# Attention and channel mix on one core: the right operands of scores and products read in another order of 16-byte lines, and the weights moved to other places

## The chip, the cores and the metric

The kernel runs on one core of a Trainium2 chip. The metric is device time in microseconds for one execution; the time given for a kernel is the median of several runs.

## The reference

There are 8 batches, 12 heads, 448 positions and a head size of 64; 12 heads of 64 make a model width of 768, and the hidden width is 1024. Everything is float32. Two stages follow one another:

```python
# attention, each element weighed by a sigmoid
scores = (q @ k.T) / sqrt(64) - log(448)
x = sigmoid(scores) @ v                     # then heads side by side: 8 x 448 x 768
# channel mix
xp = x shifted by one position
xk = mu_k * x + (1 - mu_k) * xp
xr = mu_r * x + (1 - mu_r) * xp
k  = relu(xk @ w_k)                         # 768 x 1024
v  = (k * k) @ w_v                          # 1024 x 768
r  = sigmoid(xr @ w_r)                      # 768 x 768
out = r * v
```

## The kernel before

**Attention.** Two heads share the 128 partitions, 64 each, so that there are 48 head pairs. Keys of a pair are taken in three chunks of 128 and a tail of 64. A score matmul has 128 keys of one head as weights (64 rows by 128 columns) and 448 queries as the right operand, the one that is streamed through the array; the two heads of a pair stand in the two halves of the array's rows and run side by side. Queries and keys are split in two parts each, of type fp32r (`qh`, `ql`, `kh`, `kl`), and a chunk is the sum of three terms: `kh` with `qh`, `kl` with `qh`, `kh` with `ql` (L361). The very first chunk, the key tails (L376), the products with v (L402, L412) and their tails (L426) use plain float32 operands; such a product has two records in the trace.

**Channel mix.** There are three matrix products (stage R with `w_r`, stage K with `w_k`, stage V with `w_v`), each done as seven half-size products (Strassen's scheme, `ORDER` is the order of the seven). All of their matmuls are issued from one line, L670. Weights are 128 by 128 blocks out of `slots`, seven tiles of 3072 numbers per partition, one for each of the seven; the upper part stands in the first half of a slot, the lower part in the second. Right operands are 512 (at the end of a row of blocks, 256) columns out of `rr` and later also out of `qh` and `ql`, again as an upper and a lower part (`operand`, L594 and L595). A full step takes three terms for each block of weights: upper with upper, upper with lower, lower with upper; a narrow step (`small`) takes 512 columns, in which upper and lower stand side by side, with the upper weights, and 256 with the lower ones. Weights are filled by `to_slot` (stage R) and `load_weight` (stages K and V): ACT rounds into the upper part, DVE subtracts into the lower.

**Order.** All work is put down as a list of operations with a cost and a due time. `Plan.order` runs a small list scheduler over it and writes out the instructions of each engine in the order found. Its price for a matmul is `mm(n, cols) = n * (cols / 2.4 + 13.4)` ns. Semaphores are added afterwards. `gap` reserves bytes between tiles and is otherwise unused.

The lines that place the tiles that matter here:

```python
slots = ring(base, "slot", 7, [P, 2 * WO], F32R)      # 2 * WO = 3072
rr = ring(base, "rr", 6, [P, 2, T], F32R)             # T = 512
...
qhr = ring(apool, "qh", LEAD, [P, T], F32R)
qlr = ring(apool, "ql", LEAD, [P, T], F32R)
gap(apool, "gap2", 192)
kh = ring(apool, "kh", LEAD, [P, KW], F32R)           # KW = 384
```

Of the kernel before, what the change touches and what calls it, by code (L numbers as in the profile page):

```python
# [9 lines left out]
F32R = mybir.dt.float32r  # L10
# [13 lines left out]
class Plan:  # L24
# [9 lines left out]
    def op(self, engine, cost, prio, run, reads, writes, dma=None, gate=False, opens=None):  # L34
        i = len(self.ops)
        deps = set()
        for r in reads:
            if r in self.writer:
                deps.add(self.writer[r])
        for w in writes:  # L40
            if w in self.writer:
                deps.add(self.writer[w])
            deps.update(self.readers.get(w, ()))
        for r in reads:
            self.readers.setdefault(r, []).append(i)
        for w in writes:
            self.writer[w] = i
            self.readers[w] = []
        deps.discard(i)
        self.ops.append(Op(engine, cost, prio, run, deps, dma, gate, opens))  # L50
# [58 lines left out]
def attention_then_channel_mix(  # L109
# [15 lines left out]
    nc = tc.nc  # L125
    P = 128
# [15 lines left out]
    WO = NJH * DF // 2  # L142
    SCALE = 1.0 / math.sqrt(D)
    NEG_LOG_S = -math.log(S)
    R_, K_, V_ = range(3)

    KT = (NJH, NJH, NFH)
    CW = (DM // 2, DF // 2, DM // 2)
# [18 lines left out]
    WK_PACE, WV_PACE = 1.5, 1.5  # L167
    CAST_DVE = lambda n, a: n % 2 == 1 or n == 2

    WHOLE = 1  # L170
    ZEROS = 336
    Q_FIRST = 256

    def ring(pool, name, bufs, shape, dtype):
        return [pool.tile(shape, dtype, name=f"{name}{i}") for i in range(bufs)]

    def gap(pool, name, size):
        pool.tile([P, size // 4], F32, name=name)

    base = ctx.enter_context(tc.tile_pool(name="base", bufs=1, side="left"))  # L180
    apool = ctx.enter_context(tc.tile_pool(name="apool", bufs=1, side="right"))
# [1 line left out]
    pav = psa.enter_context(tc.tile_pool(name="pav", bufs=1, space=PSUM))  # L183
    pscore = psc.enter_context(tc.tile_pool(name="pscore", bufs=1, space=PSUM, side="right"))

    slots = ring(base, "slot", 7, [P, 2 * WO], F32R)
    rr = ring(base, "rr", 6, [P, 2, T], F32R)
    ys = ring(base, "ys", 3, [P, T], F32)
    wraw = ring(base, "wraw", 2, [P, WP, 2], U32)
# [5 lines left out]
    vnr = ring(apool, "vn", 5, [P, T], F32)  # L195
    gap(apool, "gap1", 64)
    qnr = ring(apool, "qn", RAW, [P, T], F32)
    qhr = ring(apool, "qh", LEAD, [P, T], F32R)
    qlr = ring(apool, "ql", LEAD, [P, T], F32R)
    gap(apool, "gap2", 192)  # L200
    kh = ring(apool, "kh", LEAD, [P, KW], F32R)
    kl = ring(apool, "kl", LEAD, [P, KW], F32R)
    gap(apool, "gap3", 64)
# [11 lines left out]
    sc = ring(pscore, "sc", 3, [P, 2, 512], F32)  # L215
# [8 lines left out]
    def mm(n, cols):  # L224
        return n * (cols / 2.4 + 13.4)

    def act(n, sbuf=False, ptr=False):
        return 100 + 0.834 * n + 42 * sbuf + 93 * ptr

    def dve(n, fast=False, ptr=False):  # L230
        return 135 + n / (1.92 if fast else 0.96) + 61 * ptr
# [7 lines left out]
    def dma(dst, src, prio, reads, writes, e="SP"):  # L239
        ns = dst.shape[0] * math.prod(dst.shape[1:]) * 4 / 300  # L240
        q_ = nc.scalar if e == ACT else nc.sync
        op(e, 500, prio, lambda: q_.dma_start(dst, src), reads, writes, dma=ns)
# [26 lines left out]
    def convert_seven(w, t, half_rows, n, pace, at, put):  # L269
# [32 lines left out]
        combine(sub, s4, a12, s2, at + 3 * pace)  # L302
        put(2, s4, at + 3 * pace)

    def to_slot(t, n):
        def put(p, a, at):
            g = POS[p]
            hi, lo = (slots[g][:, half * KT[R_] * n + t * n:half * KT[R_] * n + (t + 1) * n] for half in range(2))
            K = ("slot", g, t)
            op(ACT, act(n, True), at, lambda: nc.scalar.copy(hi, a[0]), [a[1]], [K], gate=True)  # L310
            op(DVE, dve(n), at, lambda: nc.vector.tensor_sub(lo, a[0], hi), [a[1], K], [K + ("lo",)])
        return put
# [18 lines left out]
    def prepare(n, at):  # L331
        i = n % LEAD
        k0 = WHOLE * P if n == 0 else 0
        for src, hi, lo, a, w in ((kn[n % RAW][:, k0:KW], [t[:, k0:] for t in kh], [t[:, k0:] for t in kl], "k", KW - k0), (qn[n % RAW], qh, ql, "q", S)):
# [6 lines left out]
    half = [slice(h * D, (h + 1) * D) for h in range(2)]  # L341

    def pe(cost, go, reads, writes, at, opens=None):
        op(PE, cost, at, go, reads, writes + ["order"], opens=opens)
# [3 lines left out]
    def scores(n, c, u, at):  # L348
        i, m = n % LEAD, n % RAW
        mark = (n, c) in ((N - 1, 1), (N - 2, 2), (N - 1, 2))  # L350
        if n == 0 and c < WHOLE:
            pairs, cost, reads = ((knr[m], qnr[m]),), 752, [("kn", m), ("qn", m)]
        else:
            pairs, cost = ((kh[i], qhr[i]), (kl[i], qhr[i]), (kh[i], qlr[i])), 602
            reads = [(a, i) for a in ("kh", "kl", "qh", "ql")]

        def go(lo, hi):
            for e, (kk, qq) in enumerate(pairs):
                for h in range(2):
                    w = T if mark and e == len(pairs) - 1 else hi  # L360
                    nc.tensor.matmul(sc[u][:, h, lo:w], kk[half[h], c * P:(c + 1) * P], qq[half[h], lo:w], start=e == 0, stop=e == len(pairs) - 1, skip_group_check=mark)  # L361

        keys = [("sc", u, 0), ("sc", u, 1)]
        if (n, c) == (0, 0):

            pe(cost * Q_FIRST / S, lambda: go(0, Q_FIRST), reads, keys, at)
            pe(cost * (1 - Q_FIRST / S), lambda: go(Q_FIRST, S), reads + [("qn", 0, 1)], keys, at)
            return
        pe(cost + 2 * SWITCH * (n % 2 == c == 0), lambda: go(0, S), reads, keys, at)
# [91 lines left out]
    for t in range(KT[R_]):  # L461
        convert_seven(w_r, t, KT[R_], CW[R_], WR_PACE, WR_FROM + 4 * WR_PACE * t + 0.4, to_slot(t, CW[R_]))
# [68 lines left out]
    e = N % RAW  # L531
# [96 lines left out]
    def load_weight(stage, p, at):  # L628
        g, src = POS[p], {K_: wk_o, V_: wv_o}[stage][p]
        n = WO // 2  # L630
        for h in range(2):
            u = nw[0] % len(wop)
            nw[0] += 1
            w, W = wop[u]
            dma(w, src[:, h * n:(h + 1) * n], at, [("wo", id({K_: wk_o, V_: wv_o}[stage]), p, t) for t in range(NFH)], W)
            hi, lo = (slots[g][:, a * WO + h * n:a * WO + (h + 1) * n] for a in range(2))
            K = ("slot", g, h)
            op(ACT, act(n, True), at, lambda hi=hi, w=w: nc.scalar.copy(hi, w), W, [K])  # L638
            op(DVE, dve(n), at, lambda hi=hi, lo=lo, w=w: nc.vector.tensor_sub(lo, w, hi), W + [K], [K + ("lo",)])  # L639

    def slot_keys(g):
        return [("slot", g, h) + x for h in range(3) for x in ((), ("lo",))]
# [3 lines left out]
    def multiply(stage, s, p, i, at, cols=slice(0, T), b=None, turn=0):  # L646
        g = POS[p]
        b = b or (yb if p in (5, 6, 3) else xb)[i]
        c = cols.stop - cols.start
        rs_ = used[stage, s, p]  # L650
        w = CW[stage]
        small = PAIRS[s][1] < T

        def go():
            n = len(rs_)

            def left(t, a):
                return slots[g][:, a * n * w + t * w + i * P:a * n * w + t * w + (i + 1) * P]

            if small:  # L660

                a = turn ^ (p in (1, 6, 3))
                terms = [(left(t, a), r[0], (T, SMALL)[a]) for t, r in enumerate(rs_)]
            else:
                terms = [(left(t, a), r[e][:, cols], c) for t, r in enumerate(rs_) for a, e in ((0, 0), (0, 1), (1, 0))]
            for e, (l, r, m) in enumerate(terms):
                nc.tensor.matmul(b[0][:, :m], l, r[:, :m], start=bool(p in (0, 4) and e == turn == 0), stop=e == len(terms) - 1 and bool(turn or not small), skip_group_check=True)  # L670

        cost = mm(len(rs_), (T, SMALL)[turn ^ (p in (1, 6, 3))]) if small else mm(3 * len(rs_), c)
        op(PE, cost, at, go, [k for r in rs_ for k in r[2:]] + slot_keys(g), [b[1]])
# [87 lines left out]
    for step, (stage, s, p) in enumerate(steps):  # L761
# [6 lines left out]
        small = PAIRS[s][1] < T  # L768
        for i in range(rows if small else 0):
            multiply(stage, s, p, i, at + unit * i / (2 * rows))  # L770
        for i in range(rows):
# [9 lines left out]
            if step == len(steps) - 3 and i == rows - 1:  # L781
                a, b = yb[i], yb[NFH - 1]
# [45 lines left out]
```

## Time and profile before

| | |
|---|---|
| median of 3 runs | 803.23 us (803.14 to 803.63) |
| span of the profiled execution, first to last instruction | 801.9 us |
| TensorE matmul busy | 797.8 us, 99% |
| TensorE weight load busy | 598.8 us, 75% |
| VectorE busy | 639.7 us, 80% |
| ScalarE busy | 496.0 us, 62% |
| mean granted TensorE clock | 0.999 of full speed |

The profiled execution is one of its own beside the three timed ones; only its span is recorded, and the median of the timed runs is 1.3 us above it. Busy time of an engine is the union of its instructions. Matmuls overlap one another in the records, since each is recorded from its issue to its last result: what one matmul takes from the next is the distance of their starts.

### The profile page before, as it was taken

What the parts mean: (1) busy time and instruction counts of PE and PEld (TensorE: products, weight loads), DVE (VectorE), ACT (ScalarE), POOL (GpSimd) and SP (SyncE); (2) the same over time, 40 slices, a digit from 0 to 9 for tenths busy, and PEclk for the clock granted to TensorE, in tenths of its full rate; (3) what the DMA queues carried; (4) which work ended last, traced back from release to release, by engine and by line L of the source; (5) the groups of instructions that cost most, each with busy time, mean ns of one, the idle gap of its engine ahead of it and who ended that gap; (6) DMA issues with size and microseconds to landing.
All of it is one profiled execution on the core that took longest, in us unless ns stands there. A gap on an engine that the chain in (4) does not pass through costs nothing.

```text
span 801.9 us, 14343 instructions
## 1 busy us (share of the span) xinstructions
PE 797.8 (99%) x4935; PEld 598.8 (75%) x4935; DVE 639.7 (80%) x1210; ACT 496.0 (62%) x870; POOL 2.9 (0%) x33
## 2 busy tenths in 40 slices
PE   9999999999999999999999999999999999999998
PEld 5555555555556888888888888888888888888887
DVE  4889888898898998899987974668597585677955
ACT  6788888877785555568766464567773434345431
POOL 0000000000000000000000000000000000000000
PEclk9999999999999999999999999999999999999999
DMA  8977978789887967668877772445775564457505
GB/s 276 282 262 243 304 242 275 254 274 340 295 293 272 313 236 218 228 238 257 277 243 223 243 256 87 162 151 155 226 243 179 172 184 131 132 166 253 186 23 176
DMA packets 105336, 179.74 MB, mean 224 GB/s; under 512 B 11952, under 2 KB 58800, under 8 KB 105264
## 3 DMA queue, kind: packets, MB, share of 16 engines
q1 hardware_dynamic: 104976, 178.61, 68.9%
q8 instruction: 39, 0.64, 0.3%
q14 instruction: 33, 0.27, 0.1%
q10 hardware_dynamic: 288, 0.23, 0.1%
HBM read 109.06 MB, written 69.73 MB: 223 GB/s over the span
## 4 chain that ended last, share of the span: by engine, by line
PE 99%; DVE 0%; issue 0%
PE pb L670 69%; PE av L402 13%; PE sc L361 10%; PE sc L376 2%; PE av L426 2%; PE av L361 2%; PE av L412 1%; PE sc L445 0%; DVE vn L720 0%
## 5 line engine op out<-in xcount | busy, mean ns | idle before, releaser
L670 PE MATMUL pb<-rr,slot 128*128 128x512 f32 (+1 forms) x1908 | 440.3, 379 | 0.0
L670 PEld LDWEIGHTS pb<-rr,slot 128*128 128x128 f32 x1908 | 348.0, 188 | 68.5 <-issue 0.8
L670 PE MATMUL pb<-qh,slot 128*128 128x512 f32 (+1 forms) x468 | 154.7, 374 | 0.0
L402 PE MATMUL av<-pf,vn 64*64 64x448 f32 x1104 | 118.1, 540 | 0.0
L391 ACT ACTIVATE pf<-sc 128x896 f32<-128x896 f32 x120 | 104.0, 962 | 0.5 <-PE sc L361 0.5
L670 PEld LDWEIGHTS pb<-qh,slot 128*128 128x128 f32 x468 | 86.2, 188 | 15.8
L402 PEld LDWEIGHTS av<-pf,vn 64*64 64x64 f32 x1104 | 41.4, 132 | 56.9 <-issue 36.1
L670 PE MATMUL pb<-ql,slot 128*128 128x512 f32 (+1 forms) x177 | 68.4, 387 | 0.0
L594 ACT CAST rr<-ys 128x512 fp32r<-128x512 f32 (+1 forms) x56 | 30.9, 568 | 35.7 <-PE pb L670 34.1
L361 PE MATMUL sc<-qh,kh 64*128 64x448 f32 x238 | 46.2, 384 | 0.0
L728 ACT COPY pb<-pb 128x512 f32<-128x512 f32 x40 | 22.6, 575 | 34.5 <-PE pb L670 31.5
L361 PE MATMUL sc<-ql,kh 64*128 64x448 f32 (+1 forms) x238 | 43.4, 361 | 0.0
L436 ACT COPY xx<-av 128x448 f32<-128x448 f32 x48 | 23.3, 539 | 32.3 <-PE av L402 26.5
L361 PE MATMUL sc<-qh,kl 64*128 64x448 f32 x238 | 43.2, 359 | 0.0
L437 DVE TENSOR_TENSOR dx<-xx 128x448 f32<-128x448 f32 x48 | 29.9, 623 | 16.6 <-ACT xx L436 16.4
L595 DVE TENSOR_TENSOR rr<-pf,rr 128x512 fp32r<-128x512 f32 (+1 forms) x40 | 23.0, 608 | 20.5 <-ACT rr L594 20.5
L670 PEld LDWEIGHTS pb<-ql,slot 128*128 128x128 f32 x177 | 33.2, 188 | 6.7
L595 DVE TENSOR_TENSOR rr<-ys,rr 128x512 fp32r<-128x512 f32 (+1 forms) x56 | 33.6, 620 | 3.4 <-ACT rr L594 3.1
L361 PEld LDWEIGHTS sc<-qh,kh 64*128 64x128 f32 x238 | 22.4, 185 | 18.5 <-issue 15.5
L595 DVE TENSOR_TENSOR rr<-vn,rr 128x512 fp32r<-128x512 f32 (+1 forms) x48 | 29.6, 626 | 7.7 <-ACT rr L594 7.4
L594 ACT CAST rr<-vn 128x512 fp32r<-128x512 f32 (+1 forms) x48 | 26.9, 571 | 10.4 <-PE pb L670 8.8
L639 DVE TENSOR_TENSOR slot<-pf,slot 128x768 fp32r<-128x768 f32 x28 | 26.8, 956 | 7.8 <-ACT slot L638 7.6
(160 smaller groups left out, 1071.8 us busy)
## 6 DMA issues: line engine op xcount, KB each, us to landing
vn<-in_v SPq DMA_DIRECT2D x48, 224.0 KB, 4.3
xr_d<-mr SPq DMA_DIRECT2D x48, 224.0 KB, 4.5
xk_d<-mk SPq DMA_DIRECT2D x48, 224.0 KB, 4.3
kn<-in_k SPq DMA_DIRECT2D x47, 224.0 KB, 3.9
qn<-in_q SPq DMA_DIRECT2D x47, 224.0 KB, 4.2
wraw<-in_moe_w_k SPq DMA_DIRECT2D x12, 512.0 KB, 5.8
wraw<-in_moe_w_v SPq DMA_DIRECT2D x16, 384.0 KB, 3.7
k_d<-pt SPq DMA_DIRECT2D x23, 256.0 KB, 3.1
```

The lines of the kernel that those rows point to most:

```text
L361: nc.tensor.matmul(sc[u][:, h, lo:w], kk[half[h], c * P:(c + 1) * P], qq[half[h], lo:w], start=e == 0, stop=e == len(pairs) - 1, skip_grou ...
L376: nc.tensor.matmul(sc[u][half[m % 2], h, :S], kn[m % RAW][half[h], KW:], qn[m % RAW][half[h], :], start=True, stop=True)
L391: op(ACT, 815, at, lambda: nc.scalar.activation(f, sc[u][:, :, :S], AF.Sigmoid, bias=NEG_LOG_S, scale=SCALE), R, K, opens=opens)
L402: nc.tensor.matmul(av[m % 2][half[h], :w], vn[m % 5][half[r], h * NC + c, :], pfr[(m * NC + c) % PFB][half[r], h, :w], start=(turn, c) == ...
L426: nc.tensor.matmul(av[r][half[h], :w], vn[(n + h) % 5][half[r], 2 * NC, :], ptr[n // 2 % PTB][half[r], h, :w], start=False, stop=stop, ski ...
L436: op(ACT, act(S), at - 1, lambda: nc.scalar.copy(x[:, 1:], av[n % 2][:, :S]), [AV[n % 2]], [X])
L437: op(DVE, dve(S), at, lambda: nc.vector.tensor_sub(d, x[:, 1:], x[:, :S]), [X], [G])
L594: op(ACT, act(w, True), at, lambda: nc.scalar.copy(hi, y[:, :w]), [Y], [H], gate=True)
L595: op(DVE, dve(w), at, lambda: nc.vector.tensor_sub(lo, y[:, :w], hi), [Y, H], [L])
L639: op(DVE, dve(n), at, lambda hi=hi, lo=lo, w=w: nc.vector.tensor_sub(lo, w, hi), W + [K], [K + ("lo",)])
L670: nc.tensor.matmul(b[0][:, :m], l, r[:, :m], start=bool(p in (0, 4) and e == turn == 0), stop=e == len(terms) - 1 and bool(turn or not sma ...
L728: op(ACT, act(T), at, lambda: nc.scalar.copy(y(), x()), [X], [Y])
```

## The change

The right operand and the output of every score matmul (but those of the first chunk) and of every channel-mix matmul are given as a pattern of three levels in place of a plain run of columns. A line is four numbers, 16 bytes. With one line to a group the columns are visited as lines 0, 4, 8, ..., then lines 1, 5, 9, ..., then 2, 6, ... and 3, 7, ...; with two lines to a group as pairs of lines at a step of 8 lines; with four, as fours at a step of 16. One line is used for score chunk 0 and stage R, two for chunk 1 and stage K, four for chunk 2 and stage V. Every column is still computed once and lands where it landed before.

Slots grow by 36 numbers (9 lines), and the weights of a stage start 0, 1 or 6 lines into their slot, so that the seven slots begin at different lines. A gap of 48 bytes is put between `slots` and `rr`; a gap of 32 bytes ahead of `qh` is taken from `gap2` behind `ql`. Number, shape and type of the instructions stay.

```diff
+    LINE = 4
+    FROM = (0, LINE, 6 * LINE)
+    GROUP = (1, 2, 4)
...
-    slots = ring(base, "slot", 7, [P, 2 * WO], F32R)
+    slots = ring(base, "slot", 7, [P, 2 * WO + 9 * LINE], F32R)
+    gap(base, "gap0", 48)
...
+    gap(apool, "gap5", 32)
     qhr = ring(apool, "qh", LEAD, [P, T], F32R)
     qlr = ring(apool, "ql", LEAD, [P, T], F32R)
-    gap(apool, "gap2", 192)
+    gap(apool, "gap2", 160)
...
+    def by_lines(t, lines):
+        return t.rearrange("p (a b c) -> p b a c", b=4, c=lines * LINE)
+
+    def part(stage, g, a):
+        n = KT[stage] * CW[stage]
+        return slots[g][:, FROM[stage] + a * n:FROM[stage] + (a + 1) * n]
...
-                    nc.tensor.matmul(sc[u][:, h, lo:w], kk[half[h], c * P:(c + 1) * P], qq[half[h], lo:w], start=e == 0, stop=e == len(pairs) - 1, skip_group_check=mark)
+                    out_, right_ = sc[u][:, h, lo:w], qq[half[h], lo:w]
+                    if len(pairs) > 1:
+                        out_, right_ = by_lines(out_, GROUP[c]), by_lines(right_, GROUP[c])
+                    nc.tensor.matmul(out_, kk[half[h], c * P:(c + 1) * P], right_, start=e == 0, stop=e == len(pairs) - 1, skip_group_check=mark)
...
-                nc.tensor.matmul(b[0][:, :m], l, r[:, :m], start=bool(p in (0, 4) and e == turn == 0), stop=e == len(terms) - 1 and bool(turn or not small), skip_group_check=True)
+                nc.tensor.matmul(by_lines(b[0][:, :m], GROUP[stage]), l, by_lines(r[:, :m], GROUP[stage]), start=bool(p in (0, 4) and e == turn == 0), stop=e == len(terms) - 1 and bool(turn or not small), skip_group_check=True)
```

`to_slot`, `load_weight` and `left` in `multiply` take their slices from `part` in place of the slot itself.

## Rows read from the trace of the kernel before

**Rows 1.** The page: span, busy times, and the chain that ended last.

```profile
span 801.9 us, 14343 instructions
PE 797.8 (99%) x4935; PEld 598.8 (75%) x4935; DVE 639.7 (80%) x1210; ACT 496.0 (62%) x870; POOL 2.9 (0%) x33
...
PE 99%; DVE 0%; issue 0%
```

**Rows 2.** The chain in order of time: start us, length us, line, instructions.

```profile
24.13 2.25 PE av L402 x24
...
28.40 1.80 PE sc L361 x18
...
246.29 552.32 PE pb L670 x2553
```

**Rows 3.** Windows for L670 alone, one for each stage.

```profile
core 0: us, PE busy (x) PEld busy (x), PEclk, DMA share, GB/s
246.29:397.50 151.21, 151.21 (x695) 126.21 (x696) 1.00 0.76 253
397.50:597.50 200.00, 200.00 (x924) 167.21 (x923) 1.00 0.62 199
597.50:798.60 201.10, 201.09 (x938) 168.45 (x936) 1.00 0.52 162
```

**Rows 4.** Groups of matmuls by line and shape: busy us, mean ns of one.

```profile
L670 PE MATMUL pb<-rr,slot 128*128 128x512 f32 x1722 | 414.0, 389 | 0.0
L670 PE MATMUL pb<-qh,slot 128*128 128x512 f32 x403 | 141.3, 389 | 0.0
L670 PE MATMUL pb<-ql,slot 128*128 128x512 f32 x173 | 67.3, 389 | 0.0
L361 PE MATMUL sc<-qh,kh 64*128 64x448 f32 x238 | 46.2, 384 | 0.0
...
L670 PE MATMUL pb<-rr,slot 128*128 128x256 f32 x186 | 29.3, 283 | 0.0
...
L361 PE MATMUL av<-qh,kh 64*128 64x448 f32 x48 | 9.0, 372 | 0.0
```

**Rows 5.** Timeline of TensorE in stage K and at narrow steps of stage V.

```profile
499.80 3.56 PE L670 MATMUL pb<-rr,slot 128*128 128x512 f32 x15
...
718.89 0.40 PE L670 MATMUL pb<-rr,slot 128*128 128x256 f32 x2
719.12 0.40 PE L670 MATMUL pb<-qh,slot 128*128 128x256 f32 x2
719.36 0.40 PE L670 MATMUL pb<-rr,slot 128*128 128x512 f32 x1
```

**Rows 6.** Timeline of score matmuls, then of weight loads, about 120 us.

```profile
119.92 0.36 PE L361 MATMUL sc<-qh,kl 64*128 64x448 f32 x2
120.12 0.36 PE L361 MATMUL sc<-ql,kh 64*128 64x448 f32 x2
...
119.92 0.19 PEld L361 LDWEIGHTS sc<-ql,kh 64*128 64x128 f32 x2
120.41 0.21 PEld L402 LDWEIGHTS av<-pf,vn 64*64 64x64 f32 x8 [0.30 <-ACT pf L391]
```

**Rows 7.** The page: the costliest group of weight loads.

```profile
L670 PEld LDWEIGHTS pb<-rr,slot 128*128 128x128 f32 x1908 | 348.0, 188 | 68.5 <-issue 0.8
```

**Rows 8.** Windows of all engines: attention, then parts of stages R, K, V.

```profile
core 0: us, PE busy (x) PEld busy (x) DVE busy (x) ACT busy (x) POOL busy (x), PEclk, DMA share, GB/s
7.00:246.29 239.29, 239.26 (x2359) 133.23 (x2351) 210.12 (x421) 189.53 (x283) 2.27 (x23) 1.00 0.87 282
300.00:400.00 100.00, 100.00 (x471) 83.84 (x470) 90.63 (x174) 67.22 (x136) 0.00 (x0) 1.00 0.75 245
```

More of the change, by code (lines that the diff above doesn't have):

```diff
@@ L307, in put @@
             g = POS[p]
-            hi, lo = (slots[g][:, half * KT[R_] * n + t * n:half * KT[R_] * n + (t + 1) * n] for half in range(2))
+            hi, lo = (part(R_, g, half)[:, t * n:(t + 1) * n] for half in range(2))
             K = ("slot", g, t)
@@ L635, in load_weight @@
             dma(w, src[:, h * n:(h + 1) * n], at, [("wo", id({K_: wk_o, V_: wv_o}[stage]), p, t) for t in range(NFH)], W)
-            hi, lo = (slots[g][:, a * WO + h * n:a * WO + (h + 1) * n] for a in range(2))
+            hi, lo = (part(stage, g, a)[:, h * n:(h + 1) * n] for a in range(2))
             K = ("slot", g, h)
@@ L657, in left @@
             def left(t, a):
-                return slots[g][:, a * n * w + t * w + i * P:a * n * w + t * w + (i + 1) * P]
+                return part(stage, g, a)[:, t * w + i * P:t * w + (i + 1) * P]
             if small:
```

## The prediction, made before the changed kernel ran

> **What bounds the kernel now.** I read the page first: TensorE is busy for 797.8 of 801.9 us, and the chain that ended last is TensorE to 99% with nothing else to speak of [rows 1]. No engine and no transfer is waited for, so the time is a sum of matmul distances, and the only question is whether the change moves the distance from one matmul to the next. The chain in order of time gives these distances, because a piece of it ends where the next begins: the channel mix is one piece of 552.32 us with 2553 matmuls; 18 score matmuls, nine pairs that run side by side, take 1.80 us, so 200 ns a pair; 24 plain float32 records, six rounds of four, take 2.25 us, so 375 ns a round [rows 2]. The granted clock is 1.00, the upper of the two levels (2.4 GHz), in every stage [rows 3], so a column costs 0.4167 ns.
>
> Against the columns that they stream, these distances leave a remainder. A score pair has 448 columns, 186.7 ns, and takes 200: 13.3 ns too many. Fifteen matmuls of 512 columns in a row take 3.56 us with the last one's 389 ns tail, so (3560 - 389) / 14 = 226.5 ns each against 213.3: 13.2 too many [rows 4, 5]. Two narrow matmuls of 256 columns start 0.23 to 0.24 us before the next two, 118 ns each against 106.7: 11 to 12 too many [rows 5]. A float32 round has 448 columns at two cycles, 373.3 ns, and takes 375: only 1.7 too many [rows 2]. So each fp32r matmul carries about 13.3 ns that the float32 products don't, whatever its number of columns: 32 cycles. Over the channel mix that is 552.3 less (2298 x 213.3 + 255 x 106.7 = 517.4), 34.9 us [rows 2, 4]; over the 429 score pairs of the three-term chunks (48 x 3 - 1 chunks, 3 terms; the trace has 238 + 48 = 286 matmuls for one term, two for each of 143 chunks [rows 4]) 429 x 13.3 = 5.7 us. This 40.6 us is all that another order of reading could give back.
>
> **The change part by part.** 2553 channel-mix matmuls and 858 score matmuls get the new pattern, 3411 of 4935. No instruction is added or taken, the list scheduler's costs are the same numbers, so the order on every queue is the same, and no wait or DMA is added.
>
> *The order of reading.* Two streams read the weights' and the right operand's memory at the same time: the weights of the next matmul are loaded beside the running one, start to start 188 ns for a 128 by 128 block [rows 7]. 128 weights are 32 lines of 16 bytes in each partition, and 32 cycles is what a matmul has too many: it fits a theory in which each line of weights takes one cycle from the right operand, and then the order and the places could matter. What speaks against it is the last score matmul of a turn. The matmul at 119.92 us has the next weights loaded beside it from 119.92 on; the one at 120.12 has none beside it, since the next load starts at 120.41, after an idle 0.30 us waiting for ACT. Both are recorded with 0.36 us [rows 6]. With 0.013 us gained the second would read 0.35. The ends of matmuls in such records are modelled, so this is weak, but it goes with the other hint, that the remainder is the same for two quite different relations of places: in scores the weights stand 4 lines off the right operand modulo 16 (by the tile sizes: 2 KB and 1.5 KB tiles, and gaps of 64 and 192 bytes), in the channel mix 0 lines off. Two plain streams at two speeds (a load has 32 lines in up to 188 ns, the operand 32 lines in 53) must overtake each other in any order of banks, and yet the remainder is equal. I take the remainder as a fixed price for changing weights of this type, which no order of columns touches: the change is worth 0 here. The bounds: at best the remainder falls to the 1.7 ns of the float32 rounds, 11.6 x (2553 + 429) = 34.6 us less; a loss has no bound from a row that is near, the farthest being the two cycles for a column of the float32 rounds [rows 2].
>
> *The output's pattern.* Results are now written in runs of 4, 8 or 16 columns with a jump after each. Every number is added to what is there, at the pace of one column a cycle. No row shows a jump. Nothing at best; I take nothing, since a run is never shorter than the line that the change is built on, and price the jumps among the rivals.
>
> The Trainium skill speaks against this part: PSUM — Partial Sum Buffer, Specifications (TRN2), says that PSUM has 8-byte cachelines and that any access pattern that isn't contiguous slows matmuls significantly. By that the sum would be well over 803 us, without it it is 803; no row of this trace has such a pattern to agree or disagree.
>
> *The places of the weights.* Slots move by up to 36 numbers each. The ACT and DVE work that fills them keeps its shape; if it took longer, TensorE would hide it, which waits for none of it: DVE, the fuller of the two, is at 91% in the fullest part of stage R [rows 8]. As a load starts with the running matmul [rows 6], takes 188 ns and is wanted after 226 [rows 5, 7], it has 38 ns before it is late. What is late then is the next matmul, and behind it everything. I take 0.
>
> *The gaps.* They add bytes only. By the sizes the move of `qh` and `ql` puts them on multiples of 256 bytes. 12432 bytes of a slot are no multiple of 32; if the allocator rounds up to that, `rr` lands on an odd multiple of 128 bytes and the places of the weights come out other than meant. By the sum this costs nothing either way.
>
> The sum is 0 on the span of 801.9 us, and with the 1.3 us by which the median stands above the span, 803.2 us.
>
> **The rivals.** *A, faster:* the 32 cycles are lines of weights in the way of lines of the operand, and an operand that keeps to a quarter of the places at a time meets fewer. For it: 32 lines and 32 cycles. Against it: rows 6, the equal remainder at two relations of places, and that weights at so many places would meet good and bad relations by turns. All of the remainder over 1.7 ns gone gives 768.6; half of it, the likelier size with three patterns of which one may be right, gives 786. Between these only DVE comes near a limit: 90.63 us busy in 100 [rows 8] becomes 95 in a stage 5% shorter, no bound yet.
>
> The Trainium skill has a lower price for the remainder: TensorE: Matmul & The Clock Gate, Wait — 56ns, not 53.3ns?, gives about 2.5 ns fixed for each warm matmul. By an estimate from that page A at its best would give 10.8 x 2982 = 32 us and end near 771; the rows here show 13.3 for fp32r and 1.7 for float32.
>
> *B, slower:* jumps cost, in the output or in reading. It has a run of 4 columns in stage R, 8 in K, 16 in V. At one cycle for each jump a full matmul has 128, 64 or 32 cycles more; with 630, 840 and 828 of them and 63, 84 and 108 narrow ones with half as many jumps (by the loops; rows 3 and 4 agree) that is 35.3, 23.5 and 11.8 us, with 11.6 for the scores (112, 56, 28 jumps, 141, 144, 144 pairs): 82 us, 885. A fourth of a cycle gives 824. It decides from one cycle in fifty jumps on (1.6 us). If short runs halved the pace outright, stage R alone would lose 141 us. For it: no row has shown such a pattern; against it: none shows a price.
>
> *C, slower:* weights at places not met before stand in the way of the operand, or the reverse. A cycle for each of 32 lines at every matmul is 13.3 x 2982 = 39.8 us, 843; at a third of the places, 816. Against it are the same two hints as against A.
>
> **How the numbers follow.** A difference of under 0.2%, 1.6 us, can't be told from no change here. No change has 0.45: the hints against two streams in each other's way are weak one by one but point the same way. A has 0.24, B 0.19, C 0.12. So faster 0.24, same 0.45, slower 0.31. The likeliest gives 803.2, and its own range is 801.6 to 804.8. The range is to reach into both sides: down to 781, where A has taken back 22 of its 34.6 us, and up to 836, where B costs four tenths of a cycle for each jump or C 26 cycles in a matmul. Beyond these I leave some 0.07 below and 0.12 above.
>
> **What would show it.** If I am right, the timeline has matmuls of 512 columns still 226.5 ns apart in all three stages and score pairs 200 ns apart for all three chunks, and the three windows stay at 151, 200 and 201 us. A shows as a distance that falls towards 215 in some stages or slots and not in others, with loads still at 188 ns. B shows as distances that order by the run: R longest, V least, and chunk 0 over chunk 2, the same for all seven slots. C shows as distances that differ by slot within one stage. The prediction fails if a fixed price isn't what the 32 cycles are, or if the pattern has a price that no row here could show.

## The result, and the profile after

The changed kernel takes 814.62 us (median; 814.4 to 814.97) against 803.34 us for the kernel before on the same chip: 1.0139 times as long, 95% interval 1.0125 to 1.0154. The forecast was no change; the change makes the kernel 1.4% slower. The spans of the timed runs before are 801.2 us for a time of 803.34, so the profiled execution before, with 801.9 us, is 0.7 us longer than usual, and the profiles differ by 10.4 us where the medians differ by 11.3.

The page of the changed kernel, with the chain that ended last, answers to [rows 1]:

```profile
span 812.3 us, 14360 instructions
PE 808.2 (99%) x4935; PEld 600.1 (74%) x4935; DVE 639.5 (79%) x1210; ACT 496.1 (61%) x870; POOL 2.9 (0%) x33
...
PE 99%; DMA 0%; ACT 0%; DVE 0%; SPq 0%; issue 0%
```

TensorE has the same 4935 matmuls and is busy 10.4 us longer; the span has grown by those 10.4 us too. PEld, DVE and ACT stand where they stood, and the chain is still TensorE alone. So no wait came in: the matmuls themselves lie further apart. The chain in order of time says where (start us, length us, line, instructions), beside [rows 2]:

```profile
23.47 2.25 PE av L417 x24
...
27.75 1.84 PE sc L376 x18
...
246.55 562.54 PE pb L685 x2553
```

The 2553 channel-mix matmuls take 562.54 us instead of 552.32, 10.2 of the 10.4 us. Nine score pairs take 1.84 us instead of 1.80, and attention ends 0.3 us later. A float32 round, which the change doesn't touch, takes 2.25 us for six as before.

The windows of line 685, one for each stage (columns as in [rows 3]), split the 10.2 us:

```profile
246.48:396.15 149.67, 149.67 (x693) 125.47 (x694) 1.00 0.76 254
396.15:599.88 203.73, 203.73 (x926) 167.87 (x925) 1.00 0.61 197
599.88:809.10 209.22, 209.20 (x937) 169.37 (x935) 1.00 0.50 156
```

The windows of [rows 3] have round ends. Measured as these are, from the first matmul of one stage to that of the next, the stages before were 150.9, 200.58 and 200.61 us (the last one to the start of its last matmul). So stage R, read in single lines, gains 1.2 us; K, in pairs, loses 3.1; V, in fours, loses 8.3 (208.92 by the same measure). The granted clock is 1.00 throughout. Averaged over each stage, 512-column matmuls start 225.4, 230.7 and 236.9 ns after one another; before, it was 226.8 to 227.0.

The timeline of TensorE in stage K (start us, length us) shows one more thing. These are three runs of 45 matmuls; 36 of each come from one slot, another one in each run:

```profile
411.34 10.64 PE L685 MATMUL pb<-rr,slot 128*128 128x512 f32 x45
...
453.68 10.88 PE L685 MATMUL pb<-rr,slot 128*128 128x512 f32 x45
...
478.28 10.48 PE L685 MATMUL pb<-rr,slot 128*128 128x512 f32 x45
```

In the kernel before, the same three runs have one length in the same view, of which the first is:

```profile
412.08 10.36 PE L670 MATMUL pb<-rr,slot 128*128 128x512 f32 x45
```

Take off the last matmul's 0.39 us tail and divide by 44: 226.6 ns three times before; 233, 238 and 229 ns after. The distance now depends on the stage (the order of reading) and, within a stage, it differs from slot to slot (so with the place of the weights). The loads themselves haven't changed: the page's group of weight loads still has 188 ns, as in [rows 7]:

```profile
L685 PEld LDWEIGHTS pb<-rr,slot 128*128 128x128 f32 x1908 | 348.6, 188 | 75.2 <-issue 0.8
```

### The profile page after: what moved, and what is told of

It is laid out like the page before. It is cut to its first block, busy times and chain, and to the rows that moved or that the text cites. A ratio compares the mean times of both kernels' runs of the same rounds, so it can differ in the third digit from the quotient of the medians.

```text
span 812.3 us, 14360 instructions
## 1 busy us (share of the span) xinstructions
PE 808.2 (99%) x4935; PEld 600.1 (74%) x4935; DVE 639.5 (79%) x1210; ACT 496.1 (61%) x870; POOL 2.9 (0%) x33
## 4 chain that ended last, share of the span: by engine, by line
PE 99%; DMA 0%; ACT 0%; DVE 0%; SPq 0%; issue 0%
PE pb L685 69%; PE av L417 13%; PE sc L376 10%; PE av L441 2%; PE sc L391 2%; PE av L376 2%; PE av L427 1%; DMA kn<-in_k 0%; ACT qh L239 0%; DVE vn L735 0%; SPq L247 0%; ACT kh L239 0%
## 5 line engine op out<-in xcount | busy, mean ns | idle before, releaser
L685 PE MATMUL pb<-rr,slot 128*128 128x512 f32 (+1 forms) x1908 | 447.6, 382 | 0.0
L685 PE MATMUL pb<-qh,slot 128*128 128x512 f32 (+1 forms) x468 | 156.4, 378 | 0.0
```

The costliest lines, as they stand in the source:

```text
L685: nc.tensor.matmul(by_lines(b[0][:, :m], GROUP[stage]), l, by_lines(r[:, :m], GROUP[stage]), start=bool(p in (0, 4) and e == turn == 0), s ...
```

## The experiments

A line is four numbers, 16 bytes, as in the kernel's `LINE`. A place is the line, modulo 16, at which a block of weights starts, counted from where the right operand starts: 0 in the channel mix before. "Plain" is the order before; singles, pairs and fours are the change's three orders of reading, each in four passes over the operand. All ratios are against the kernel before on the same chip.

### Order and places apart

The change has two halves. e1_places keeps its places and reads plainly; e2_order keeps the places of before and reads in the new orders.

```
e1  def by_lines(t, lines): return t               # the rest as in the changed kernel
e2  FROM = (0, 0, 0); slots, gap0, gap5, gap2 as before; by_lines as in the change
```

> The places of after with the plain order of columns. Theory 1 (the weight load and the operand's reading get in each other's way line by line, and the order of lines decides how often): plain order overtakes the load in the same way from any place, so the matmuls stay 226.7 ns apart in every slot and the time is 803.3 us. Theory 2 (jumps in the output cost): 803.3 us, since nothing jumps. Theory 3 (the places alone do it): 814.6 us as after, and distances that differ by slot.

> The three orders of after with slots, gaps and first lines of before, so weights and operand of the channel mix begin at the same line modulo 16 everywhere. Theory 1: stage R near 225 ns a matmul, stage V near 238, stage K between; 812 to 817 us. Theory 2: 814.6 us, as after. Theory 3: 803.3 us.

e1: 816.28 us, 1.0159 [1.0142, 1.0176]. e2: 817.04 us, 1.0167 [1.0152, 1.0182]. Each half alone costs about 13 us, and together they cost 11.3: they don't add. The timeline of e1 for the three runs of 45:

```profile
416.36 10.55 PE L685 MATMUL pb<-rr,slot 128*128 128x512 f32 x45
...
458.65 10.66 PE L685 MATMUL pb<-rr,slot 128*128 128x512 f32 x45
...
483.05 10.58 PE L685 MATMUL pb<-rr,slot 128*128 128x512 f32 x45
```

And that of e2, whose three runs again have one length:

```profile
412.14 10.54 PE L683 MATMUL pb<-rr,slot 128*128 128x512 f32 x45
```

With the places of before all slots are alike again, at 230.7 ns in K (226.6 in R, 239.5 in V). So the order sets a level for a stage. With the new places and the plain order the slots differ, and all lie above 226.6: 231 to 233 in these rows, 227 to 234 over all. An operand read in plain order is not indifferent to where the weights start, as Theory 1 of e1 had it.

### Output and operand apart

```
e3  matmul(by_lines(b[0][:, :m], GROUP[stage]), l, r[:, :m], ...)
e4  matmul(b[0][:, :m], l, by_lines(r[:, :m], GROUP[stage]), ...)   # both with e2's places
```

> Places of before, the operand read in plain order, only the output written by the three orders; the columns of a result then land in a permuted order, so the result is not the reference's. Theory 1: 803.3 us, 226.7 ns a matmul in all three stages. Theory 2: 812 to 817 us, and the distances of e2_order stage by stage.

> Places of before, only the operand read by the three orders, the output written plainly; the columns land permuted, so the result is not the reference's. Theory 1: the distances and the time of e2_order to within 0.3 us. Theory 2: 803.3 us.

e3: 803.33 us, 0.9998 [0.9989, 1.0007]. e4: 816.46 us, 1.016 [1.0145, 1.0175], the whole of e2. The channel mix in e3's chain, then in e4's:

```profile
245.89 551.84 PE pb L683 x2552
```

```profile
246.66 88.91 PE pb L683 x396
335.60 475.99 PE pb L683 x2157
```

Jumps in the output, after runs of 4, 8 or 16 columns, cost nothing. The Trainium skill's rule that a pattern that isn't contiguous slows matmuls significantly (PSUM — Partial Sum Buffer, Specifications (TRN2)) is not borne out for runs of these lengths. All of it comes from reading the right operand.

### Distances by themselves

m1_pairs is a row of matmuls with no waits. It reads one operand with one block of weights, 18 or 12 times for each of some 200 pairings, and each pairing has a line of its own. Its outputs are zeros.

```
for i in range(18): matmul(b[i % 4], W[:, 12:140], by(X[:, :512], 1, 1))   # plain, place 3
for i in range(18): matmul(b[i % 4], W[:, 12:140], by(X[:, :512], 4, 1))   # singles, place 3
for i in range(12): matmul(b[i % 4], W[:, 12:13].to_broadcast([P, 128]),
                           X[:, 0:4].unsqueeze(1).to_broadcast([P, 128, 4]))  # one line, one number
```

> A measurement by itself: matmuls of 128 by 128 weights and 512 columns, fp32r, one after the other with nothing else running, and zeros as output; it leaves out all of the reference's computation. Each line of the program is one pairing of a right operand's order (plain, groups of 1, 2, 4 or 8 lines in four passes, single lines in 2, 8 or 16 passes, and two others) with weights that begin 0 to 15 lines after the operand, and then an operand of one line and a weight of one number read over and over, 0 to 31 and more lines apart. Theory 1, refined (memory is interleaved by lines over banks, and the two streams wait for one another where they meet in a bank): the pairs of one line and one number show two prices, a high one at 0 and at each multiple of the number of banks (4, 8 or 16) and about 216 ns at the rest; orders with plain weights lie between 216 and 245 ns and change with the place. Theory 4 (the 13.3 ns is a fixed price of changing fp32r weights, and orders only add to it): no pairing is under 226 ns, also where the two read one line each.

The chain of m1 in order of time: each piece ends where the next begins, so length by count is the distance.

```profile
16.29 4.08 PE b L50 x18
20.37 4.09 PE b L51 x18
...
28.65 4.20 PE b L53 x18
...
95.22 3.96 PE b L69 x18
...
123.69 4.17 PE b L76 x18
...
214.32 4.30 PE b L98 x18
...
487.97 4.98 PE b L162 x18
...
712.19 2.62 PE b L213 x12
...
820.20 2.78 PE b L254 x12
836.57 2.63 PE b L260 x12
```

Lines 50, 51 and 53 are plain at places 0, 1 and 3: 226.7, 227.2, 233.3 ns. Over all 16 places plain gives 226.7 to 227.2 at 0, 1 and 15, and 229.4 to 234 elsewhere. Lines 69 and 76 are singles at places 3 and 10: 220.0 and 231.7. Line 98 is fours at 0: 238.9. Line 162 takes single lines in 16 passes, so from one line to the sixteenth after it: 276.7. Line 213 rereads one line of the operand, with weights that are one number spread out: 218.3. Line 254 has the same weights and a plain operand, 231.7; line 260 ordinary weights and one line of operand, 219.2.

This table is found again in e1. By the tile sizes, rounded up to 32 bytes, its second slot stands at place 0 in stage R and the other six at other even places, where m1 has 226.7 ns and 233 to 234; by the starts in e1's trace the second slot takes 227.2 ns and the others 231.6 to 233.9.

So the price of 13.3 ns over the columns is not fixed, as Theory 4 had it. It is 5 to 6 ns when the operand stays on one line, whichever the weights, and up to 63 ns by how it steps. Theory 1's two prices aren't there either: one line of operand against one number takes 218.5 to 218.8 ns at all 41 places. The 5 ns are twice the 2.5 ns fixed for a warm matmul that the Trainium skill gives (TensorE: Matmul & The Clock Gate, Wait — 56ns, not 53.3ns?).

### Singles at the best place

The best pairing, singles at place 3, goes into the kernel in e5_singles_at3 for all three stages, with the scores read as before. e7_singles_at0 takes the same order at the places of before.

```
AHEAD = 3 * LINE;  GROUP = (1, 1, 1);  FROM = (0, 0, 0)
every = base.tile([P, 14 * WO + AHEAD], F32R, name="slots")
slots = [every[:, AHEAD + g * 2 * WO:AHEAD + (g + 1) * 2 * WO] for g in range(7)]
gap(base, "gap0", 192)                            # e7: slots and gaps as before
```

> All three stages read single lines in four passes, and all seven slots begin 3 lines after the operands modulo 16 (one tile holds the slots); scores as before. Theory 1 (the price is set by the order together with the place): as in the pair measured by itself, 220.0 ns a matmul, 6.7 ns less on 2298 of them, 788 us. Theory 5 (pairs by themselves run into a rhythm that mixed operands, narrow steps and waits in the kernel break): about 225 ns as stage R of the order alone, 800 us or more.

> As e5_singles_at3 but at the places of before, slots and operands at the same line modulo 16. Theory 1: between the 222.9 ns of the pair by itself and the 226.6 ns of stage R of the order alone, 795 to 803 us, in any case slower than at 3. Theory 5: 803 us, the same as at 3.

e5: 786.83 us, 0.9794 [0.978, 0.9809]. e7: 795.72 us, 0.9901 [0.9885, 0.9918]. Both times lie where Theory 1 expected them. But e7 hasn't one distance: by the starts in its trace 512-column matmuls lie 226.6 ns apart in stage R and in K up to its narrow steps, and 223.3 after them. e5's stage windows for line 686:

```profile
245.46:391.86 146.40, 146.36 (x693) 125.61 (x694) 1.00 0.77 259
391.86:586.48 194.62, 194.62 (x926) 167.27 (x925) 1.00 0.63 206
586.48:781.40 194.92, 194.85 (x937) 167.69 (x935) 1.00 0.53 168
```

The three runs of 45 have 10.06 us each in e5's timeline:

```profile
406.38 10.06 PE L686 MATMUL pb<-rr,slots 128*128 128x512 f32 x45
```

That is 220 ns. At this place the rate that one operand and one block showed holds with all operands and slots.

e6_singles_scores reads the scores in single lines too. Its three chunks are all read by singles (`GROUP` is (1, 1, 1) there), not by 1, 2 and 4 lines as its expectation says.

```
-                    if False:
+                    if len(pairs) > 1:
```

> As e5_singles_at3, with scores read in the orders of after (groups of 1, 2 and 4 lines by chunk) at the key places of before, 12 lines after the queries. Theory 1: of the pairs measured, 12 lines after gives 222 ns for single lines, 226 for pairs of lines and 238 for fours, so of the three chunks two gain or stay and one loses; 0 to 2 us more than e5_singles_at3. Theory 5: about 2 us more.

786.43 us, 0.9786 [0.9772, 0.9801]: it can't be told from e5. Nine score pairs fall from 1.80 to 1.74 us, but the products behind them, which the edit doesn't touch, get longer. These are the same two pieces in the chain of e5 and in that of e6:

```profile
97.96 1.80 PE sc L377 x18
...
101.42 1.50 PE av L418 x16
```

```profile
98.22 1.74 PE sc L377 x18
...
101.63 1.59 PE av L418 x16
```

By the starts over 22 turns of 36 score and 64 float32 matmuls, the scores take 1.9 us less in all and the float32 matmuls 1.3 us more, so that the channel mix starts at 245.36 us instead of 245.53 by the chains of the two. In half of these turns the first product that is late starts 53 ns after the end of ACT's last sigmoid; in e5 103 to 118 ns lie between the two. There, TensorE has come too early for ACT. What makes the products longer in the other turns is open.

### Which of the change's own parts decides

e9_after_singles changes one line of the changed kernel, so that all is read in singles at the change's places. e10_after_aligned moves `rr`, which had come to stand at an odd multiple of 128 bytes, to multiples of 256. e11_singles_at10 is e5 with the weights at place 10 instead of 3.

```
e9    -    GROUP = (1, 2, 4)            +    GROUP = (1, 1, 1)
e10   -    gap(base, "gap0", 48)        +    gap(base, "gap0", 176)     # and no gap4
e11   -    AHEAD = 3 * LINE             +    AHEAD = 10 * LINE          # gap0 96
```

> After, with single lines in all stages and chunks in place of one, two and four. Theory 1 (order and place together set the price): stages K and V fall to the 225 ns that stage R has at its seven slots, 840 x 5 + 828 x 11.5 ns less, and the scores gain a little: 800 to 802 us, level with before or just under it, and far from the best place. If groups of two and four were not the reason that after is slower: 814 us.

> After, with the operands in rr moved by 128 bytes onto multiples of 256 bytes, as the change means them to be (the gap behind the attention tiles is left out to make room). Theory 1: other slots get the good and the bad places, the mean over seven slots stays, 811 to 818 us. If the operands' own alignment were what counts: clearly less than 814 us, in stage K and V too.

> As e5_singles_at3, the same orders and the same tiles, but all seven slots begin 10 lines after the operands. Theory 1: as in the pair measured by itself, 231.5 ns a matmul, 4.8 ns more than before on 2298 of them, 812 to 815 us. If single lines alone made e5_singles_at3 fast: 787 us.

e9: 798.57 us, 0.9943 [0.9926, 0.9959]. e10: 816.41 us, 1.0162 [1.0147, 1.0177]. e11: 801.22 us (799.8 to 802.83), 0.9973 [0.9961, 0.9984]. e9's stage windows for line 685:

```profile
245.15:394.69 149.54, 149.54 (x694) 125.52 (x695) 1.00 0.76 254
394.69:593.30 198.61, 198.61 (x925) 167.18 (x924) 1.00 0.62 201
593.30:792.90 199.60, 199.59 (x937) 167.62 (x935) 1.00 0.52 164
```

R stays as in the changed kernel, K falls by 5.1 us and V by 9.6. So the pairs and the fours are what makes the change slower, and without them it would be 0.6% faster than before, 1.4 us under what was expected. Where `rr` stands is not the cause. Between e11 and e5 only the place differs, and it is worth 14.4 us. But e11 was expected slower than before, at 812 to 815 us, and is 0.3% faster: it has 227.0 ns on average where m1 had 231.7 for that pairing. Two runs of 54 matmuls in e11's stage R, one before its narrow steps and one after them, show why:

```profile
295.78 12.67 PE L686 MATMUL pb<-rr,slots 128*128 128x512 f32 x54
...
373.42 12.31 PE L686 MATMUL pb<-rr,slots 128*128 128x512 f32 x54
```

That is 231.7 and 224.9 ns. By the starts in the trace, the first distance, which is m1's, holds for R up to the narrow steps (333 to 355 us), the second from there through K, and the first again behind the narrow steps of V (710 to 739 us). So one pairing of order and place can have two steady distances, and which one holds depends on what ran before.

### What carries the price

m2_lines lets the operand go to and fro between two lines, or step over fresh lines, beside weights that are one number at each of 16 places; m3_parties varies how many columns the weights and the operand have. Both compute nothing of the reference, as m1.

```
m2  alt(16):  64 times (line 0, line 16)          step(s): 128 lines, each s lines after the last
m3  matmul(b[i % 4][:32, :], W[:, 12:44], by(X[:, :512], 1, 1))     # 32 columns of weights, plain
    matmul(b[i % 4], W[:, 12:13].to_broadcast([P, 128]), by(X[:, :512], 4, 4))   # one number, fours
```

> A measurement by itself, zeros as output, none of the reference's computation: an operand that goes to and fro between two lines 1, 2, 3, 4, 8 or 16 apart, or steps by 2, 4, 8 or 16 lines, against a weight of one number 0 to 16 lines away; then single lines in four passes with two operands in turn at 0 to 15 lines; then score pairs of 64 rows and 448 columns, plain and in groups of 1, 2 and 4, at 0 to 15 lines. Theory 1a (the streams meet in banks of lines): the two-line operands are dear where the weight's line falls in the bank of one of the two, at distances that repeat with the number of banks, and 218.7 ns elsewhere. Theory 1b (an operand that leaves a line pays for the line itself, whatever the weights read): the price of a two-line operand depends on how far its lines are apart, not on the weight's place. For the scores: plain and groups of 1 between 195 and 205 ns a pair, with a best place for groups of 1.

> A measurement by itself, zeros as output, none of the reference's computation: the operand's orders against a weight load that reads one number over and over; then loads of 32, 64, 96 and 128 columns of weights at six places, plain, single lines and fours; then operands of 128 to 512 columns. Theory 1c (lines of the load and lines of the operand get in each other's way): with one number as weights single lines and fours cost the same at every place, and the price over 218 ns shrinks with the number of weight columns, to a fourth at 32. Theory 1d (the operand's walk carries the price, and the place only shifts its start): the price over 218 ns is the same for 32 and for 128 columns of weights and grows with the number of the operand's columns.

m2's chain, for to and fro 16 lines apart, then for steps of 2, 4, 8 and 16 lines:

```profile
210.16 2.18 PE b L147 x10
...
256.94 2.31 PE b L168 x10
...
297.43 2.47 PE b L185 x10
...
337.60 2.57 PE b L201 x10
...
386.24 2.87 PE b L219 x10
```

218 ns, then 231, 247, 257 and 287. To and fro is cheap (218 to 219 ns) at every distance from 1 to 16 lines, at every place of the one number, so neither Theory 1a nor 1b holds. Steps over fresh lines get dearer with the step, and again the place of the one number makes next to no difference (for the step of 8, 255 to 263 ns). m3's chain has, at place 3, plain, singles and fours with one number for weights (lines 51, 57, 69), then plain, singles and fours with 32 columns of weights (87, 111, 135), and plain and singles with all 128 (105, 129):

```profile
20.97 4.62 PE b L51 x20
48.50 4.48 PE b L57 x20
103.28 4.75 PE b L69 x20
...
194.25 4.63 PE b L87 x20
277.23 4.66 PE b L105 x20
304.97 4.45 PE b L111 x20
384.75 4.42 PE b L129 x20
412.17 4.75 PE b L135 x20
```

Plain is 231 ns with one number, 231.5 with 32 columns and 233 with 128. Singles are 224, 222.5 and 221, fours 237.5 with one number and with 32 columns. For plain and fours a quarter of the weights doesn't bring a quarter of the price, as Theory 1c had it: it is the operand's own walk over its lines that costs, and a full load only shifts it, by -4 to +7 ns according to its place (m1's 16 places against m3's one number, all four orders). Singles are another case, which place 3 hides. Over m3's six places they have 224 ns on average with one number for weights, 227 with 128 columns and 220 with 32, where three of the six have 216.7, less than an operand that stays on one line. So in singles the load has a large share, and of the two theories neither holds for all orders. The price grows with the operand's columns: plain matmuls lie 10 to 15 ns over the columns' own time with 256 columns, 13 to 17 with 384, 13 to 21 with 512.

## Why the prediction was wrong

The 814.62 us lie inside the stated 781 to 836, but that is the width of the rivals: the likeliest value, 803.2 with a range of its own from 801.6 to 804.8, is missed by 11.4 us.

*What bounds the kernel: right.* TensorE's distances set the time before and after, no wait came in, and the 10.4 us are matmul distances at a granted clock of 1.00.

*The order of reading: the step that failed.* "I take the remainder as a fixed price for changing weights of this type, which no order of columns touches: the change is worth 0 here." The remainder isn't fixed: m1 has it from 6 to 63 ns with the same number of columns and a full block of weights at both ends (lines 260 and 162). The order alone makes 1.0167 (e2), all of it from the operand (e4). By the runs, the step should have had three prices, by stage: 225.4, 230.7 and 236.9 ns against 227.

The two hints that it rested on were weak in ways that can now be named. The records of [rows 6] have modelled ends: in the changed kernel they read 0.38 to 0.41 us while the starts lie 217 to 247 ns apart, so 13 ns more or less could not show in them. And the "equal remainder at two relations of places" came from two good ones: m1 has plain products at 226.7 ns at the channel mix's place 0, with up to 234 at others; m2 has plain score pairs at about 200 ns at place 12, the scores' relation (4 lines off), with up to 206 at others. The remainder of 13.3 was near a minimum twice, not a constant. "Whatever its number of columns" was no support either: at place 0 it comes out nearly so (m3 has 13 to 15 ns for 256 columns and 14 for 512 there), but at the other places it is 10 to 13 against 18 to 21.

*The output's pattern: right*, nothing, e3 0.9998.

*The places of the weights: wrong.* At 0 they were costed by the time of a load alone. That part held: 188 ns, never late (the 188 of [rows 7] is the length of a load, not its distance from start to start, but no sum uses it as such). But the places cost 1.0159 with the plain order (e1), and 14.4 us between e5 and e11.

*The gaps: right.* `rr` did come to an odd multiple of 128 bytes, by the tile sizes and by where the good slot lies in e1, and putting it right gained nothing (e10).

*The rivals.* A's gain existed, up to 0.9786 in e6, and the change took some of it in stage R only. A's mechanism of weight lines in the way is refuted for plain and fours (m3: a quarter of the weights, the same price); for singles it isn't, since there narrower loads do make the price smaller. B had the sign and its reason partly: reading out of order has a price. But the output has none, and its order by run is turned round, since the longest runs (V) are dearest. C was a true cause by itself, and showed as it said, in distances that differ by slot, but at 13 us it is well under C's 40. That C's 816, for a third of the places, is e1's time is chance: in e1 512-column matmuls lie 5 ns further apart on average, not 13.3 at a third of the places.

*What stays open.* What inside a walk over lines costs the time isn't settled: singles in four passes are cheaper than plain, pairs about equal to it, fours dearer, and none of the theories tried gives these three sizes. Nor is it settled how the place of a load shifts them, why narrower loads help singles alone, and what picks one of two steady distances: e11 and e7 change theirs at narrow steps, and singles at place 13 have 223 ns with one operand in m1 and 231.2 with two in turn in m2. So what ran just before matters, and a table of pairings measured one at a time gives a good choice but not always its size.

## What to carry to other kernels

A remainder that is the same in all the kernel's conditions isn't thereby a fixed price: ask whether the conditions differ in what could set it, and measure it alone, in a kernel of a few hundred short rows of matmuls with a source line for each pairing, so that the chain reads off all distances at once. Test a change of order and a change of places each by itself before putting them together, since here each cost 13 us and both together 11. When a kernel is all TensorE, the best pairing so found can be tried in it at once, and its distance read there, since it may be another one (e11): single lines in four passes with the weights 3 lines after the operand took 803.45 to 786.83 us.

## What the hardware showed that was not expected

With the same 512 columns of fp32r, matmuls start from 217 to 287 ns apart, by the operand's order of lines and by the weights' number and place, at a granted clock of 1.00; with a full block of weights it is 218 to 280, with loads that stay at 188 ns. Within one slot the distance isn't constant but goes in rhythms: in the changed kernel's stage R one slot repeats 234, 239, 225, 225, 220, 222, 221 ns. One pairing can have two such rhythms, 231.7 and 225 ns, and keep either for hundreds of matmuls (e11). And a gain of 7 ns on a score pair came almost to nothing in the kernel (e6), since the products behind the scores got longer, in half of the turns because ACT's last sigmoid was then awaited.
